# A fused SSM convolution and gated MLP on one core: two spectrum spills moved from the first down phase into the next gate stage, and two chunks of the third gate stage left without convolution steps

## The chip, the core and the metric

The kernel runs on one core of a Trainium2 chip. The metric is the time of one execution on the device in microseconds (us), as a median of several runs. The profile is that of one such execution, taken by the hardware profiler, and it has its own time.

The engines are named as the profile names them: PE is the matrix engine (PEld its weight loads), DVE the vector engine, ACT the scalar engine, POOL the general engine, SP the engine whose instruction queue issues nearly all DMA transfers (SPq in the profile). Each runs its own instructions in order, and they wait for each other through semaphores.

## What is computed

Sequence length 2048, width 576, MLP width 4608, bfloat16 data. Two residual blocks follow one another, both with a layer norm whose scale and shift come from a conditioning vector:

```python
h = layernorm(x) * (1 + ca) + sa
# A: k is shifted and mixed over 4 taps, kv = k_shift * v, then a long causal convolution
y = irfft(rfft(pad(kv)) * rfft(pad(ssm_k)))[:S] + kv * ssm_D
x = x + ga * (h * y)
h = layernorm(x) * (1 + cb) + sb
# B: a gated MLP
x = x + gb * ((silu(h @ w1) * (h @ w3)) @ w2)
```

The convolution is done in blocks of 256 rows, eight of them: block s of the output is a sum over i of (spectrum X of kv block i) times (spectrum V of filter block s - i). The MLP works on four row blocks of 512 rows, each of two convolution blocks.

## The kernel before

**The stages.** `row_blocks` goes over the row blocks r = 0 to 3. For each it runs a gate stage (`stream`; for the last row block `stream_halves`) and then a down phase (`down`). The gate stage computes h @ w1 and h @ w3 for 36 chunks of 128 hidden columns (L1018 and L1029 on PE), puts silu and the copy of the other half on ACT (L1036, L1040) and multiplies them on DVE (L1043). The result lies in `h3`. The down phase multiplies `h3` with w2 (L1139) in two halves of 288 output columns, nine blocks of four hidden chunks in each half, and DVE scales and adds the result to the rows (L1164, L1165).

**The convolution beside it.** While row block r goes through its MLP, the convolution of row block r + 1 is worked off as a list of small steps (the generator `conv`). After each gate chunk, `hide` calls `advance` with a cost, and after each w2 block `down` does so too; `advance` takes as many steps off the list as the sum of the costs allows. In the second half of the down phase (`TURN`), `end` takes all that is left, and the normed rows `h2row` are then transposed by two DMA transposes (L823) into `h2T`, scaled (L838, or L836 on DVE), and are what the next gate stage multiplies with. A layer of the compiler orders the instructions of all engines by their place in the program, so that a step taken later stands later in each engine's queue.

**Spectra.** X (three buffers) and V (four buffers) of the old blocks stay in on-chip memory as long as there are buffers, and are spilled to DRAM for later row blocks: `keep_x(i)` (L446) and `keep_v(i)` (L450) write 864 KB each, `get` (L463) reads one back into the next free buffer. A buffer that is to be used again waits for its last reader and for its spill. In the first down phase of before, four spills are issued, one behind every fourth w2 block: V3, V2, X2, X3. X1, V0 and V1 follow in the gate stage of r = 1, each with the weight load of a group of four chunks (the dictionary `spills`, its keys are those groups).

**Queues.** The w1 and w3 weights (`load_w13`, L969 and L970, 512 KB and 64 KB), the w2 blocks (L1128, 288 KB), spills, reloads, rows and transposes all go through SP's queue. A w2 block goes into one of four places, so its issue waits until PE has done with the block four before it. Each DMA uses one of eight semaphores in turn, so that its issue also waits for the landing of the DMA that used the same one before. Below, w2 blocks of a down phase are counted 0 to 17 over both halves; T1 and T2 are the two transposes of its second half.

PSUM has four accumulators of two banks (`ps`). A gate chunk takes one until ACT has read it, a down half takes two, a spectrum step (L348, copied out by L350) takes one for a moment.

Of the kernel before, what the change touches and what calls it, by code (L numbers as in the profile page):

```python
# [27 lines left out]
W2C = 4  # L28
# [6 lines left out]
HEAD = 8  # L35
HEAD_PACE = 1.4
# [13 lines left out]
class _Kernel:  # L50
# [932 lines left out]
    def stream(self, r, jobs, rate, size, finish=False):  # L983

        nc = self.nc
        hT = self.h2T[r % 2]  # L990
        items = []
        for job in jobs:
            m = RB // (job[2] - job[1])
            items += [(job, fi, m) for fi in range(0, FC, m)]
        gus, ws = {}, {}

        def load(job):
            fc, _, _, buf, also = job
            if fc not in self.w13 and buf is not None:
                if r == 0:  # L1000
                    with self.behind(nc.sync):
                        self.load_w13(fc, buf)
                else:
                    self.load_w13(fc, buf)
            w = self.kept[fc] = self.w13.pop(fc) if buf is not None else self.kept[fc]
            ws[job[0:3]] = w
            if also is not None:
                with self.behind(nc.sync):
                    also()


        def full(k, first):
            (fc, t0, t1, _, _), fi, m = items[k]
            w, n = ws[fc, t0, t1], t1 - t0
            for a in range(m):
                for i in range(2):
                    for ct in range(4):
                        nc.tensor.matmul(gus[k][:, i, a * n:(a + 1) * n],  # L1018
                                         w[:, 5 * i + ct, (fi + a) * P:(fi + a + 1) * P], hT[:, ct, t0:t1],
                                         start=(first and ct == 0 and a == 0),  # L1020
                                         stop=(not first and ct == 3 and a == m - 1))

        def rest(k, first):
            (fc, t0, t1, _, _), fi, m = items[k]
            w, n = ws[fc, t0, t1], t1 - t0
            for a in range(m):
                for i in range(2):
                    rows = slice(64 * i, 64 * i + 64)
                    nc.tensor.matmul(gus[k][:, i, a * n:(a + 1) * n],  # L1029
                                     w[rows, 4, (fi + a) * P:(fi + a + 1) * P], hT[rows, 4, t0:t1],  # L1030
                                     start=(first and a == 0), stop=(not first and a == m - 1))

        def hide(k):
            (fc, t0, t1, _, _), fi, m = items[k]
            f = fc * FC + fi
            nc.scalar.activation(self.h3[:, f:f + m, t0:t1], gus[k][:, 0, :].rearrange("p (a t) -> p a t", a=m),  # L1036
                                 ACT.Silu)
            if k % 2 == 0:
                self.u = self.hp.tile([P, 2, RB], BF16, name="u", tag="u")
            nc.scalar.copy(self.u[:, k % 2, :], gus[k][:, 1, :])  # L1040
            if k % 2 == 1:
                h3 = self.h3[:, f - m:f + m, t0:t1]
                nc.vector.tensor_mul(h3, h3, self.u[:].rearrange("p b (a t) -> p (b a) t", a=m))  # L1043
            del gus[k]
            self.advance(rate * 2.05 * (HEAD_PACE if r == 1 and k < HEAD else 1.0))

        def begin(k):
            if items[k][1] == 0:
                load(items[k][0])
            gus[k] = self.ps()  # L1050
        for k in range(0, len(items), size):
            early, late = range(k, k + size // 2), range(k + size // 2, k + size)
            for m in early:
                begin(m)
                full(m, True)
            for m in early:
                rest(m, False)
            for m in late:
                begin(m)
                rest(m, True)  # L1060
            for m in early:
                hide(m)
            if finish and late.stop == len(items):
                self.end()
            for m in late:
                full(m, False)
                hide(m)
# [50 lines left out]
    def down(self, r, rate):  # L1118
        nc = self.nc
        for h in range(2):  # L1120

            tail = r == NRB - 1 and h == 1
            accs = [self.ps() for _ in range(4 if tail else 2)]
            acc = [accs[t][:, 0, 0:H] if tail else accs[t // 2][:, t % 2, 0:H] for t in range(4)]
            for n, fc in enumerate(FIRST if r == 0 else range(NF // W2C)):
                f0 = n * W2C
                w = _ap(self.w2m, (h * NF + f0) // W2C % NW2 * W2C * H, [[H, W2C], [1, H]])
                nc.sync.dma_start(w, self.w2[fc * W2C * P:(fc + 1) * W2C * P, h * H:(h + 1) * H]  # L1128
                                  .rearrange("(a p) d -> p a d", p=P))
                last = f0 + W2C == NF  # L1130
                if h == 0 and last:
                    self.last_w2 = self.newest()
                order = [(f, t) for f in range(W2C) for t in range(4)]
                if f0 == 0:
                    order = [(f, t) for t0 in (0, 2) for f in range(W2C) for t in (t0, t0 + 1)]
                if last:
                    order = [(f, t) for t in range(4) for f in range(W2C)]
                for f, t in order:
                    nc.tensor.matmul(acc[t],  # L1139
                                     self.h3[:, fc * W2C + f, t * P:(t + 1) * P], w[:, f, :],  # L1140
                                     start=(f0 + f == 0), stop=(f0 + f == NF - 1))
                if h == 1 and f0 // W2C == TURN and r + 1 < NRB:

                    self.end()
                    self.turn_all(2 * r + 3)
                    if 2 * r + 5 < NBLK:
                        self.pair_taps(2 * r + 5)
                    self.modulate(2 * r + 3, r > 0)
                if (f0 // W2C) % 4 == 3:

                    leave = ((self.keep_v, 3), (self.keep_v, 2), (self.keep_x, 2), (self.keep_x, 3)) if r == 0 else ()
                    for keep, i in leave[2 * h + f0 // (4 * W2C):][0:1]:
                        keep(i)
                self.advance(rate * W2C * 4 * 0.126)
            cols = slice(h * H, (h + 1) * H)
            for a in range(2):
                s = 2 * r + a
                x1 = self.xo[s]
                rows = self.out[B * s:B * (s + 1), :].rearrange("(p c) d -> p c d", c=2)
                g = self.lnp.tile([P, 2, H], BF16, name="og", tag="og")  # L1160
                for cc in ((slice(0, 1), slice(1, 2)) if tail else (slice(0, 2),)):
                    n = cc.stop - cc.start
                    ps = acc[2 * a + cc.start].unsqueeze(1) if tail else accs[a][:, :, 0:H]
                    nc.vector.tensor_mul(g[:, cc, :], ps, _ap(self.gbrow, h * H, [[0, n], [1, H]]))  # L1164
                    nc.vector.tensor_add(x1[:, cc, cols], x1[:, cc, cols], g[:, cc, :])  # L1165
                    if r == NRB - 1:
                        nc.sync.dma_start(rows[:, cc, cols], x1[:, cc, cols])
                    elif h == 1:
                        nc.sync.dma_start(rows, x1[:])
# [29 lines left out]
    def row_blocks(self, n1):  # L1199
        for r in range(NRB):  # L1200
            cost = 0
            if r + 1 < NRB:
# [3 lines left out]
                cost = CONV_US[r]  # L1206
            time = 110.0 * 0.85 - (N1 * 1.03 if r == 0 else 0)
            rate = cost / time
            if r == 0:

                jobs = [(fc, 256, 512, None, None) for fc in (n1 - 2, n1 - 1)]

                new = [(n1 + i, 0, RB, b, None) for i, b in enumerate((2, 1, 2))]
                again = [(fc, 256, 512, b, None) for fc, b in enumerate((0, 0, 1, 0))]
                while new or again:
                    jobs += new[0:1] + again[0:1]
                    new, again = new[1:], again[1:]
            else:
                spills = {1: (self.keep_x, 1), 2: (self.keep_v, 0), 4: (self.keep_v, 1)} if r == 1 else {}
                bufs = [b if b == 2 else (r + b) % 2 for b in (0, 1, 2, 0, 1, 2, 0, 1, 0)]  # L1220
                jobs = [(fc, 0, RB, bufs[fc], (lambda f, i: lambda: f(i))(*spills[fc]) if fc in spills else None)
                        for fc in range(NF // FC)]
# [59 lines left out]
```

## Time and profile before

| | |
|---|---|
| median of 5 runs | 509.38 us (508.33 to 510.9) |
| profiled execution | 508.74 us, of which the span from the first to the last instruction is 506.7 us |
| busy in the span | PE 486.8 us (96%), DVE 339.5, ACT 282.3, POOL 22.3 |
| mean granted PE clock | 0.998 |
| DMA | 107.97 MB, mean 213 GB/s |

The stages as the profile shows them, in us from the start of the span: first block and set-up to 90, gate stage of r = 0 to 122.2, its down phase to 164.2, gate stage r = 1 to 241.9, its down phase to 287.6, gate stage r = 2 to 358.4, its down phase to 396.2, then the last gate stage and down phase to the end.

How to read it: a row of the timeline is a run of equal instructions of one engine, with its start, its duration and, in brackets, the idle time before it and what ended that. A PE that is busy is not yet one at its peak, because the ends of matmuls are modelled; but in its gate stages the starts of the matmuls follow each other at a fixed step, and idle time is told in the brackets.

### The profile page before, as it was taken

What the parts mean: (1) busy time and instruction counts of PE and PEld (TensorE: products, weight loads), DVE (VectorE), ACT (ScalarE), POOL (GpSimd) and SP (SyncE); (2) the same over time, 40 slices, a digit from 0 to 9 for tenths busy, and PEclk for the clock granted to TensorE, in tenths of its full rate; (3) what the DMA queues carried; (4) which work ended last, traced back from release to release, by engine and by line L of the source; (5) the groups of instructions that cost most, each with busy time, mean ns of one, the idle gap of its engine ahead of it and who ended that gap; (6) DMA issues with size and microseconds to landing.
All of it is one profiled execution on the core that took longest, in us unless ns stands there. A gap on an engine that the chain in (4) does not pass through costs nothing.

```text
span 506.7 us, 8848 instructions
## 1 busy us (share of the span) xinstructions
PE 486.8 (96%) x3508; PEld 286.2 (56%) x3528; DVE 339.5 (67%) x448; ACT 282.3 (56%) x561; POOL 22.3 (4%) x41
## 2 busy tenths in 40 slices
PE   6999999999998999999999999999999999999996
PEld 3667775547776444343777443434677544444774
DVE  8989898897997576997067999799762321112012
ACT  5658679659243588579450455976824355555000
POOL 4200000000001000000000000000000000000000
PEclk9999999999999999999999999999999999999999
DMA  8988986849999995358799997644575554460562
GB/s 272 337 199 231 320 254 200 246 148 305 266 365 300 296 305 172 105 148 250 202 300 323 313 300 227 209 117 164 152 178 123 172 177 135 148 187 0 141 168 66
DMA packets 115036, 107.97 MB, mean 213 GB/s; under 512 B 20339, under 2 KB 107572, under 8 KB 114996
## 3 DMA queue, kind: packets, MB, share of 16 engines
q1 hardware_dynamic: 114974, 107.41, 71.7%
q8 instruction: 27, 0.44, 0.3%
q14 instruction: 13, 0.11, 0.1%
q10 hardware_dynamic: 22, 0.01, 0.0%
HBM read 92.46 MB, written 9.44 MB: 201 GB/s over the span
## 4 chain that ended last, share of the span: by engine, by line
PE 63%; DVE 17%; DMA 9%; ACT 6%; issue 3%; SPq 1%; POOL 1%; POOLq 0%; DVEq 0%; ACTq 0%
PE ps L1018 27%; PE ps L1139 14%; PE ps L1082 14%; PE ps L1029 4%; DMA wst<-in_B_w_dram 4%; DMA V<-Vd 2%; DVE p L439 2%; DMA kh<-in_A_k_dram 2%; DVE z L441 2%; ACT junk L470 2%; DVE z L434 2%; DVE og L1164 1%; PE ps L348 1%; PE ps L573 1%; DVE h L1043 1%
## 5 line engine op out<-in xcount | busy, mean ns | idle before, releaser
L1018 PE MATMUL ps<-h2T,wst 128*128 128x512 bf16 (+1 forms) x1037 | 198.8, 340 | 1.8 <-issue 0.3
L1139 PE MATMUL ps<-wst,h 128*128 128x288 bf16 x1152 | 145.4, 286 | 5.5 <-DMA wst<-in_B_w_dram 5.1
L1018 PEld LDWEIGHTS <-wst 128*128 128x128 bf16 x1056 | 100.1, 98 | 86.3 <-issue 14.5
L1139 PEld LDWEIGHTS <-h 128*128 128x128 bf16 x1152 | 112.5, 98 | 37.0 <-issue 8.5
L1036 ACT ACTIVATE h<-ps 128x512 bf16<-128x512 f32 x108 | 64.8, 600 | 78.9 <-PE ps L1029 50.8
L1082 PE MATMUL ps<-h2T,wst 64*128 64x512 bf16 x648 | 70.3, 376 | 0.0
L1040 ACT CAST u<-ps 128x512 bf16<-128x512 f32 x108 | 63.3, 586 | 0.0
L439 DVE TENSOR_TENSOR p<-X,V 128x3456 bf16<-128x3456 bf16 x28 | 54.8, 1956 | 3.9 <-DMA V<-Vd 3.4
L441 DVE TENSOR_TENSOR z<-z,p 128x3456 bf16<-128x3456 bf16 x28 | 54.7, 1954 | 0.1
L1082 PEld LDWEIGHTS <-wst 64*128 64x128 bf16 x648 | 31.3, 94 | 38.3 <-DVE og L1164 0.2
L1109 DVE TENSOR_TENSOR h<-h,u 128x1024 bf16<-128x1024 bf16 x18 | 12.5, 692 | 58.1 <-ACT u L1106 58.1
L1043 DVE TENSOR_TENSOR h<-h,u 128x1024 bf16<-128x1024 bf16 x54 | 37.0, 687 | 14.1 <-ACT u L1040 14.1
L1103 ACT ACTIVATE h<-ps 128x512 bf16<-128x512 f32 x36 | 21.5, 597 | 39.9 <-PE ps L1082 39.9
L470 ACT ACTIVATE junk<-x 128x576 bf16<-128x576 bf16 x52 | 35.7, 687 | 3.1 <-DVE x L588 2.6
L1164 DVE TENSOR_TENSOR og<-ps,gbrow 128x576 bf16<-128x576 f32 (+1 forms) x18 | 12.3, 688 | 36.9 <-PE ps L1139 36.4
L1029 PE MATMUL ps<-h2T,wst 64*128 64x512 bf16 (+1 forms) x264 | 33.5, 342 | 0.3
L1106 ACT CAST u<-ps 128x512 bf16<-128x512 f32 x36 | 20.9, 579 | 0.0
L838 ACT ACTIVATE h2T<-h2T,sbcol,cbcol 128x256 bf16<-128x256 bf16 x20 | 10.4, 589 | 18.5 <-DMA h2T<-h2row 18.5
L1029 PEld LDWEIGHTS <-wst 64*128 64x128 bf16 x264 | 8.5, 94 | 21.5 <-issue 18.6
L599 ACT ACTIVATE h2row<-x,l2n,l2r 128x576 bf16<-128x576 bf16 (+1 forms) x24 | 13.7, 642 | 10.2 <-DVE l2n L488 10.2
L368 DVE TENSOR_TENSOR kv<-kv,p 128x1152 bf16<-128x1152 bf16 x24 | 18.1, 756 | 0.3
L362 DVE TENSOR_TENSOR p<-kh,shk 128x3456 bf16<-128x3456 bf16 x8 | 15.6, 1954 | 1.2 <-DMA kh<-in_A_k_dram 1.2
(135 smaller groups left out, 361.4 us busy)
## 6 DMA issues: line engine op xcount, KB each, us to landing
wst<-in_B_w_dram SPq DMA_DIRECT2D x80, 512.0 KB, 5.1
wst<-in_B_w_dram SPq DMA_DIRECT2D x72, 288.0 KB, 3.9
wst<-in_B_w_dram SPq DMA_DIRECT2D x80, 64.0 KB, 3.4
kh<-in_A_k_dram SPq DMA_DIRECT2D x7, 720.0 KB, 6.8
X<-Xd SPq DMA_DIRECT2D x5, 864.0 KB, 5.8
V<-Vd SPq DMA_DIRECT2D x5, 864.0 KB, 5.7
Xd<-X SPq DMA_DIRECT2D x4, 864.0 KB, 8.3
Vd<-V SPq DMA_DIRECT2D x4, 864.0 KB, 5.4
```

Of the source, the lines that this page charges most:

```text
L439: nc.vector.tensor_mul(p[:], X[:], V[:])
L441: nc.vector.tensor_add(z[:], z[:], p[:])
L470: self.nc.scalar.activation(junk[:], src[:, i, :], func, scale=scale, accum_out=out[:, col:col + 1])
L1018: nc.tensor.matmul(gus[k][:, i, a * n:(a + 1) * n], w[:, 5 * i + ct, (fi + a) * P:(fi + a + 1) * P], hT[:, ct, t0:t1], start=(first and ct ...
L1029: nc.tensor.matmul(gus[k][:, i, a * n:(a + 1) * n], w[rows, 4, (fi + a) * P:(fi + a + 1) * P], hT[rows, 4, t0:t1], start=(first and a == 0 ...
L1036: nc.scalar.activation(self.h3[:, f:f + m, t0:t1], gus[k][:, 0, :].rearrange("p (a t) -> p a t", a=m), ACT.Silu)
L1040: nc.scalar.copy(self.u[:, k % 2, :], gus[k][:, 1, :])
L1043: nc.vector.tensor_mul(h3, h3, self.u[:].rearrange("p b (a t) -> p (b a) t", a=m))
L1082: nc.tensor.matmul(gus[k][:, i, :], ws[fc][rows, 5 * i + ct if ct < 4 else 4, cols], hT[rows, ct, :], start=swap == 0 and ct == 4, stop=sw ...
L1103: nc.scalar.activation(h3, gus[k][:, 0, :], ACT.Silu)
L1106: nc.scalar.copy(self.u[:, k % 2, :], gus.pop(k)[:, 1, :])
L1139: nc.tensor.matmul(acc[t], self.h3[:, fc * W2C + f, t * P:(t + 1) * P], w[:, f, :], start=(f0 + f == 0), stop=(f0 + f == NF - 1))
```

## The change

Two spills, those of V2 and X3, leave the down phase of r = 0: two of its four entries are now empty. In the gate stage of r = 1 they are issued with the weights of groups 2 and 3; V0 and V1, which were issued there with groups 2 and 4, now go with groups 5 and 6. X1 stays with group 1.

In the gate stage of r = 2, the last two chunks (34 and 35) take no steps of the convolution any more: their cost is added to the account `due`, and the first `advance` of the down phase takes those steps.

```diff
@@ hide, in stream
             del gus[k]
-            self.advance(rate * 2.05 * (HEAD_PACE if r == 1 and k < HEAD else 1.0))
+            cost = rate * 2.05 * (HEAD_PACE if r == 1 and k < HEAD else 1.0)
+            if r in (2,) and k >= len(items) - 2:
+                self.due += cost
+            else:
+                self.advance(cost)
@@ down
-                    leave = ((self.keep_v, 3), (self.keep_v, 2), (self.keep_x, 2), (self.keep_x, 3)) if r == 0 else ()
-                    for keep, i in leave[2 * h + f0 // (4 * W2C):][0:1]:
+                    leave = ((self.keep_v, 3), (), (self.keep_x, 2), (),) if r == 0 else ()
+                    for keep, i in filter(None, leave[2 * h + f0 // (4 * W2C):][0:1]):
                         keep(i)
@@ row_blocks
-                spills = {1: (self.keep_x, 1), 2: (self.keep_v, 0), 4: (self.keep_v, 1)} if r == 1 else {}
+                spills = {1: (self.keep_x, 1), 2: (self.keep_v, 2), 3: (self.keep_x, 3), 5: (self.keep_v, 0), 6: (self.keep_v, 1)} if r == 1 else {}
```

The number of instructions on every engine stays as it was. In the order of the built programs, these things move beside the edited lines:

- SP, down phase r = 0: the loads of group 1's weights begin behind w2 block 7, where they began behind block 9. X1's spill stands between blocks 10 and 11 (it stood between 11 and 12), X2's stays between 12 and 13. The end of the phase stood as block 16, two of the copies of the filter taps (`kT`, L313), X3's spill, T1, T2, block 17, and X0's reload (L463) behind it. Now it is block 15, X0's reload, block 16, T1, block 17, T2. The loads of k and v rows for the next block (L285, L291) and a filter transpose (L304), which stood behind the weights of group 2, now stand among them.
- PE, down phase r = 0: one L1018 matmul of the next gate stage stood ahead of the last 16 matmuls of the down phase; now all 128 matmuls of the last eight blocks come first.
- DVE: the product of X0 and V4 (L439, L441) moves ahead of the two evictions (L1164) that end this down phase.
- End of gate stage r = 2: on PE, the last chunk's eight L1018 and the first 16 L1139 come before two pairs of L348; on ACT, the last chunk's L1036 and L1040 come before two L534, four L470 and one L350; on SP, T1 of this down phase's first half stands behind three w2 blocks, not two.

## The prediction

> **What bounds the kernel now.** I read the page first, then the stages, then the timelines of PE and SP around the two places that the change touches.
>
> ```profile
> PE 486.8 (96%) x3508; PEld 286.2 (56%) x3528; DVE 339.5 (67%) x448; ACT 282.3 (56%) x561; POOL 22.3 (4%) x41
> ...
> L1139 PE MATMUL ps<-wst,h 128*128 128x288 bf16 x1152 | 145.4, 286 | 5.5 <-DMA wst<-in_B_w_dram 5.1
> ```
>
> PE is the bound, and its waits for w2 blocks are 5.1 us in the whole span: no change to transfers can win much more. Then the stages:
>
> ```profile
> 122.40:164.40 42.00, 38.47 (x307) 29.76 (x305) 37.33 (x44) 18.20 (x36) 2.96 (x2) 1.00 1.11 310
> 164.40:241.90 77.50, 76.97 (x385) 31.85 (x392) 60.53 (x74) 57.64 (x116) 2.50 (x3) 1.00 0.69 212
> ...
> 146.00:154.00 8.00, 5.73 (x46) 4.31 (x45) 7.42 (x10) 3.22 (x10) 2.27 (x1) 1.00 1.05 374
> ```
>
> Columns: window, length, busy time of PE, PEld, DVE, ACT and POOL, granted clock, busy share of the DMA engines, GB/s. In the first down phase DMA is full (1.11). In the gate stage behind it PE is busy for 76.97 of 77.5 us with DMA at 0.69: a time won before 164 is kept there, and a spill put there has room. PE in the down phase:
>
> ```profile
> 135.27 2.12 PE L1139 MATMUL ps<-wst,h 128*128 128x288 bf16 x16 [0.98 <-DMA wst<-in_B_w_dram]
> ...
> 149.66 2.12 PE L1139 MATMUL ps<-wst,h 128*128 128x288 bf16 x16 [0.36 <-DMA wst<-in_B_w_dram]
> 153.69 8.00 PE L1139 MATMUL ps<-wst,h 128*128 128x288 bf16 x64 [1.91 <-DMA wst<-in_B_w_dram]
> 161.97 0.38 PE L1018 MATMUL ps<-h2T,wst 128*128 128x512 bf16 x1 [0.28 <-ACT h2T L838]
> 162.24 2.12 PE L1139 MATMUL ps<-wst,h 128*128 128x288 bf16 x16
> ```
>
> Sixteen matmuls are one w2 block, 1.96 us. Counting by 16, PE waits for blocks 6 (0.98), 12 (0.36) and 13 (1.91); one gate matmul then waits 0.28 for `h2T`, and block 17 follows at 162.24. SP's queue:
>
> ```profile
> 133.02 1.55 SPq L450 DMA_DIRECT2D Vd<-V  x1
> ...
> 153.71 0.53 SPq L446 DMA_DIRECT2D Xd<-X  x1
> 155.36 2.58 SPq L823 DMA_TRANSPOSE h2T<-h2row  x2
> 158.03 0.53 SPq L1128 DMA_DIRECT2D wst<-in_B_w_dram  x1
> ```
>
> V2's spill goes out at 133.02, X3's at 153.71 right ahead of T1 and T2, block 17 last. In the same timeline block 6 is issued at 129.84 and block 13 at 145.16, 8.5 us before PE has it; the page's median for such a block is 3.9.
>
> **Part 1: two spills out of the first down phase.** The wait for block 6 stays: its load was issued 3.2 us before V2's spill. V2 takes 884,736 bytes out of the full stretch, 2.4 us at the 374 GB/s of 146 to 154. Blocks 12 and 13 must come 0.36 and 0.36 + 1.91 = 2.27 us earlier for PE not to wait. The Trainium skill (DMA: Bandwidth & Descriptors, Specifications) gives a ceiling of 435 GB/s, by which the spill is worth 2.0 and 0.3 of wait is left; by the row nothing is left. I take the row, the rate of this very stretch. (X1's spill now stands ahead of block 11, but one spill out and one in leaves its bytes as they were.) So block 16 ends at 153.69 + 8.00 - 2.27 = 159.4.
>
> Late next is block 17. It stands behind T1, which waits for the first row of `h2row`: ACT's L599 started at 153.84, at the end of a DVE chain that did not wait for w2, so it does not move. Half of its 2.29 us gives 155.0, T1's issue 1.26 more, and block 17 goes out at 156.3, not 158.03. With the 3.9 of the page it lands at 160.2, with the 5.8 of block 16 (issued 151.81) at 162.1. I take 160.4, so PE waits 1.0 here in place of 2.27 before, and its 16 matmuls end at 162.4. T2, now behind block 17, goes out at 156.9, 0.2 later than before. It took 4.58 us to land, with X3's spill just ahead; its like in the third down phase took 3.70 and 2.63 with no spill ahead. A rule of the skill speaks against a gain here (same page, Queues, rings and completion order: each DMA engine takes the descriptors of an issuing queue in ring order), so what stands ahead counts, and X0's reload, also 864 KB, comes into the place that X3's spill leaves, some 3 us earlier. By the rows without a spill T2 lands at 160.6, by the rule at 161.5. ACT scales the fourth column tile 2.1 us later, 162.7 or 163.6; PE, started at 162.4, wants it at 163.0. I take 0.3 of loss, the middle. The gate matmuls then count from 162.7; before, their second started at 164.20, so they count from 163.98. **1.3 won**; from -0.3 (block 17 and `h2T` late) to 2.2 (nothing comes in the waits' place).
>
> **What it could cost, each taken at nothing, and its cover.**
> - X0's reload waits for X2's spill (issued 143.4; X1's took 7.2 to land) and holds block 16 and T1 behind it: free at about 151, block 16's place at 151.8. Every us past that is one lost.
> - The DVE product of X0 and V4 ahead of the two evictions: 3.9 us into an idle time of 2.14, so the second eviction is 1.5 later; PE wants that accumulator for its fourth chunk, 6 us into the stage.
> - V2's spill (about 165) must land before DVE writes V5, 178.4 before; landing 5.4.
> - X3's spill stands behind the weights of group 3, whose place is free after four chunks, at 172. It goes at 173 and lands by 182 with the page's 8.3 for such a spill; ACT writes its buffer at 186.6.
> - The row loads behind those weights come at 172, not 167; ACT reads at 180.5.
> - V0 and V1 at groups 5 and 6 meet DMA at 0.69, and weights issued some 15 us before their use; nothing reads them before 250.
>
> Without its cover, ACT or DVE would stand in order and PE with it, us for us.
>
> **Part 2: the end of gate stage r = 2.**
>
> ```profile
> 357.08 1.63 ACT L534 ACTIVATE hg<-x,l1n,l1r 128x576 bf16<-128x576 bf16 x2
> ...
> 359.96 12.78 PE L1139 MATMUL ps<-wst,h 128*128 128x288 bf16 x103 [0.26 <-ACT X L350]
> ...
> 365.37 1.24 SPq L823 DMA_TRANSPOSE h2T<-h2row  x1
> ...
> 373.04 3.22 PE L1139 MATMUL ps<-wst,h 128*128 128x288 bf16 x25 [0.30 <-DMA wst<-in_B_w_dram]
> ```
>
> PE waits 0.26 for an accumulator that a spectrum copy (L350) holds behind L534 and L470 on ACT. With the spectrum matmuls behind the first 16 L1139, both accumulators of the down phase are free: 0.26 won, and the last silu, at 360.48, no longer stands behind them. No instruction is added. The same steps run later: L534 1.63, four L470 at 0.86, two L350 at 0.6 and 1.26 over DVE and POOL, from 359.3 on, put L599 at 366.7, 2.5 later than 364.14. T1 of the first half and its block 7 behind it go with that: T1 at 367.9, block 7 at 369.2. Before, block 7 was held to 369.52 by both transposes. So it lands much as before, the 0.30 at 373.04 stays, and of the 0.26 PE keeps what the earlier issue gives, 0.2. DVE's z is done half a us later, 374, for matmuls at 378.9. **0.2 won**, between -0.5 (blocks 7 and 8 both late behind the transposes) and 0.6.
>
> Sum: 508.74 - 1.3 - 0.2 = 507.2 in the profiled execution. The median, 509.38, lies 0.64 above that execution: **507.8 us**.
>
> **The rivals.**
> - *The wait only moves.* Block 17 and `h2T` end the phase however early blocks 12 and 13 are, since the `h2row` chain stands still; with 162.1 for block 17, part 1 gives nothing and the time is 509.2. For: 1.26 us of T1 stand ahead of block 17. Against: it is issued 1.7 us earlier than before.
> - *All of the w2 waits behind V2 go.* Landings of 3.9 and 3.7: 2.2 + 0.6, 506.6.
> - *X3's spill becomes ACT's wait (slower).* At about 186 ACT's copy of spectrum X4 needs X3's buffer, and silus and PSUM copies queue behind it. The spill is behind SP's waits for PE and for V2's landing. It decides from a landing after 186 + 1.5; to be 2 us slower in all (511.4) it must land at 190, 17 us after my issue time. Against: that is twice the page's 8.3.
> - *It changes nothing measurable* because the reload of X0 gives back V2's 2.4 us: 509.
>
> **How the numbers follow.** A measurement of this kernel tells about 0.3% (1.5 us) from no change, so the bounds are 507.85 and 510.9, and my sum lies on the first. Chances: the sum as worked 0.4, all waits gone 0.2, the wait moves or is given back 0.22, X3's spill or another cover that fails 0.18. Half of the first and the whole of the second give faster, 0.40; the last gives slower, 0.18; the same has 0.42. The range goes from 506.0 (the upper ends of both parts, 505.94 + 0.64 = 506.6, and 0.6 of spread, the shown runs lying within 1.5 of their median) to 510.6, which takes in the whole of the moved wait and stops short of the slower case, about 0.15, with 0.05 left out below.
>
> **What would show it.** Right: no wait at blocks 12 and 13, the 0.98 at block 6 unchanged, a wait of about 1 at block 17, the gate stage counted from 162.7, 77.5 us long as before, no wait for L350 at 360. Wrong: waits at 12 or 13 still over 0.5, T1 issued after 155.5, a PE gap between 165 and 200 behind ACT or DVE, or L599 in the third down phase later than 367 with PE waiting over 0.6 at block 7 or 8.

## The result, and the profile after

| | before | after |
|---|---|---|
| median | 508.98 us (506.87 to 511.14, 40 runs) | 505.36 us (504.33 to 508.63, 21 runs) |
| profiled execution, span | 508.74 us, 506.7 us | 505.74 us, 503.9 us |

The ratio is 0.9938, 95% interval 0.9923 to 0.9953: 3.2 us won (2.4 to 3.9). The prediction was 507.8 us with a range from 506.0 to 510.6; the measured median lies 0.6 below that range. Faster was given 0.40, the same 0.42; by the bound of 0.3% that the prediction set for itself, this is faster. The median of before, now over 40 runs, lies 0.4 under the 509.38 that the prediction counted from.

In the costliest groups of the page of after, the lines L1128, L1139 and L1164 of before are L1132, L1143 and L1168:

```profile
PE 486.2 (96%) x3508; PEld 286.0 (57%) x3528; DVE 338.9 (67%) x448; ACT 282.4 (56%) x561; POOL 22.7 (4%) x41
...
L1143 PE MATMUL ps<-wst,h 128*128 128x288 bf16 x1152 | 145.4, 286 | 3.6 <-DMA wst<-in_B_w_dram 3.5
```

PE's busy time is the same to 0.6 us and its waits for w2 blocks fell from 5.1 to 3.5. The windows by stage of after (first down phase, the gate stage behind it, and the same 8 us that the prediction took its rate from; columns as there):

```profile
121.82:160.89 39.07, 37.87 (x306) 29.72 (x304) 36.80 (x42) 17.50 (x36) 2.96 (x2) 1.00 1.12 305
160.89:238.61 77.72, 77.19 (x386) 31.89 (x392) 60.32 (x75) 58.41 (x118) 2.50 (x3) 1.00 0.74 226
146.00:154.00 8.00, 7.47 (x62) 5.83 (x61) 7.42 (x12) 3.25 (x9) 2.27 (x1) 1.00 1.10 337
```

The phase is 39.07 us and not 42.00. DMA is still full in it (1.12), so a transfer that is wanted soon can still be late there. Between 146 and 154, where PE was busy for 5.73 us of 8, it is now busy for 7.47. The gate stage is as long as before, if before is counted from 163.98 as the prediction did: 77.72 there too. PE in the first down phase, by its timeline:

```profile
121.82 11.92 PE L1143 MATMUL ps<-wst,h 128*128 128x288 bf16 x96
134.00 2.12 PE L1143 MATMUL ps<-wst,h 128*128 128x288 bf16 x16 [0.25 <-DMA wst<-in_B_w_dram]
...
143.94 8.00 PE L1143 MATMUL ps<-wst,h 128*128 128x288 bf16 x64
152.48 4.08 PE L1143 MATMUL ps<-wst,h 128*128 128x288 bf16 x32 [0.53 <-DMA wst<-in_B_w_dram]
156.97 4.08 PE L1143 MATMUL ps<-wst,h 128*128 128x288 bf16 x32 [0.42 <-DMA wst<-in_B_w_dram]
160.89 1.89 PE L1018 MATMUL ps<-h2T,wst 128*128 128x512 bf16 x7
```

The 64 matmuls at 143.94 are blocks 10 to 13 without a stop: both waits that the prediction wanted gone are gone. Smaller ones came at blocks 14 and 16. Block 17 and the first gate matmuls wait for nothing. The wait at block 6 is 0.25, not 0.98. SP's queue at the end of the phase:

```profile
149.03 1.38 SPq L463 DMA_DIRECT2D X<-Xd  x1
150.51 0.39 SPq L1132 DMA_DIRECT2D wst<-in_B_w_dram  x1
153.79 1.21 SPq L823 DMA_TRANSPOSE h2T<-h2row  x1
155.10 0.53 SPq L1132 DMA_DIRECT2D wst<-in_B_w_dram  x1
155.72 1.21 SPq L823 DMA_TRANSPOSE h2T<-h2row  x1
...
163.92 0.57 SPq L450 DMA_DIRECT2D Vd<-V  x1
```

X0's reload goes out at 149.03 (before: 160.22), T1 at 153.79 and block 17 at 155.10. The prediction had both 1.2 us later, but PE, too, is 1.27 us earlier in this profile: block 9 starts at 141.74, in before at 143.01. And the end of the third gate stage on PE:

```profile
356.19 2.12 PE L1143 MATMUL ps<-wst,h 128*128 128x288 bf16 x16
358.15 0.65 PE L348 MATMUL ps<-kv,Fb 128*128 128x288 bf16 x4
358.64 17.56 PE L1143 MATMUL ps<-wst,h 128*128 128x288 bf16 x142
```

The spectrum matmuls (L348) stand behind the first block. Neither the wait for L350 nor the one for block 7 is there any more.

**Waits counted by steps.** From here on a wait is the time from one matmul's start to the next one's, less 0.12 us for each matmul, since 16 of them take 1.96 us from start to start. That is more than the idle time in brackets: an x16 row is shown with 2.12 us where the next row can start after 1.96, so each bracket leaves out 0.16 us. The first down phase is cut at the start of block 9, since up to block 7 nothing moves in the order of SP's instructions. Lengths in us from the profiled executions ("gate" is counted 0.22 earlier where one L1018 runs ahead of the last block, as it does in before):

| kernel | start to block 9 | block 9 to gate | gate r = 1 | gate r = 2 with its down phase |
|---|---|---|---|---|
| before | 20.77 | 20.97 | 77.73 | 115.52 |
| before again (e6) | 20.26 | 21.00 | 77.72 | 115.24 |
| steps only (e2) | 20.98 | 22.28 | 77.77 | 114.65 |
| X3 only (e4) | 19.51 | 20.64 | 77.72 | 115.89 |
| V2 only (e3) | 20.17 | 18.87 | 78.61 | 115.14 |
| V2 split (e12) | 20.36 | 18.92 | 78.01 | 115.07 |
| both spills (e1) | 19.72 | 19.00 | 77.72 | 115.67 |
| no spill (e8) | 19.87 | 18.85 | 77.72 | 115.24 |
| after | 19.92 | 19.15 | 77.72 | 114.65 |
| after again (e5) | 20.00 | 18.61 | 77.88 | 114.65 |
| after, X1 too (e7) | 20.74 | 18.61 | 77.94 | 114.70 |
| after, early 17 (e9) | 20.07 | 18.93 | 77.72 | 114.74 |
| X1 too, early 17 (e10) | 19.94 | 18.07 | 77.72 | 114.70 |
| and steps r = 1 (e11) | 19.51 | 17.88 | 77.72 | 114.60 |

The profiled pair differs by 2.8 us in span. By the table: 0.85 before block 9, 1.82 from there to the gate stage, 0.87 in the stretch of part 2. The stages ahead of the change are 0.42 shorter in after, and the second down phase is 1.22 longer (it waits 2.7 us in all for w2 blocks, before 1.5). Sum: 0.85 + 1.82 + 0.87 + 0.42 - 1.22 = 2.74.

### The profile page after: what moved, and what is told of

It reads as the page before. It is cut to its first block, busy times and chain, and to the rows that moved or that the text cites. A ratio compares the mean times of both kernels' runs of the same rounds, so it can differ in the third digit from the quotient of the medians.

```text
span 503.9 us, 8848 instructions
## 1 busy us (share of the span) xinstructions
PE 486.2 (96%) x3508; PEld 286.0 (57%) x3528; DVE 338.9 (67%) x448; ACT 282.4 (56%) x561; POOL 22.7 (4%) x41
## 4 chain that ended last, share of the span: by engine, by line
PE 64%; DVE 17%; DMA 9%; ACT 4%; issue 3%; SPq 1%; POOL 0%; POOLq 0%; DVEq 0%; ACTq 0%
PE ps L1018 27%; PE ps L1143 15%; PE ps L1086 14%; PE ps L1029 4%; DMA wst<-in_B_w_dram 4%; DMA V<-Vd 3%; DVE p L439 2%; DMA kh<-in_A_k_dram 2%; DVE z L441 2%; ACT junk L470 2%; DVE z L434 2%; DVE og L1168 2%; PE ps L348 1%; PE ps L573 1%; DVE h L1043 1%
## 5 line engine op out<-in xcount | busy, mean ns | idle before, releaser
L1018 PE MATMUL ps<-h2T,wst 128*128 128x512 bf16 (+1 forms) x1037 | 198.6, 340 | 1.6 <-issue 0.3
L1018 PEld LDWEIGHTS <-wst 128*128 128x128 bf16 x1056 | 100.1, 98 | 86.8 <-issue 15.0
L1143 PE MATMUL ps<-wst,h 128*128 128x288 bf16 x1152 | 145.4, 286 | 3.6 <-DMA wst<-in_B_w_dram 3.5
L1143 PEld LDWEIGHTS <-h 128*128 128x128 bf16 x1152 | 112.5, 98 | 34.7 <-issue 5.7
L1036 ACT ACTIVATE h<-ps 128x512 bf16<-128x512 f32 x108 | 64.8, 600 | 79.0 <-PE ps L1029 49.8
L1040 ACT CAST u<-ps 128x512 bf16<-128x512 f32 x108 | 63.4, 587 | 0.0
L439 DVE TENSOR_TENSOR p<-X,V 128x3456 bf16<-128x3456 bf16 x28 | 54.7, 1955 | 3.8 <-DMA V<-Vd 3.4
L441 DVE TENSOR_TENSOR z<-z,p 128x3456 bf16<-128x3456 bf16 x28 | 54.7, 1953 | 0.1
L470 ACT ACTIVATE junk<-x 128x576 bf16<-128x576 bf16 x52 | 35.7, 687 | 3.1 <-DVE x L588 2.6
L1168 DVE TENSOR_TENSOR og<-ps,gbrow 128x576 bf16<-128x576 f32 (+1 forms) x18 | 12.3, 688 | 34.1 <-PE ps L1143 33.6
L599 ACT ACTIVATE h2row<-x,l2n,l2r 128x576 bf16<-128x576 bf16 (+1 forms) x24 | 13.8, 654 | 12.5 <-DVE l2n L488 12.5
```

Source lines behind the costliest of these rows:

```text
L439: nc.vector.tensor_mul(p[:], X[:], V[:])
L441: nc.vector.tensor_add(z[:], z[:], p[:])
L470: self.nc.scalar.activation(junk[:], src[:, i, :], func, scale=scale, accum_out=out[:, col:col + 1])
L1018: nc.tensor.matmul(gus[k][:, i, a * n:(a + 1) * n], w[:, 5 * i + ct, (fi + a) * P:(fi + a + 1) * P], hT[:, ct, t0:t1], start=(first and ct ...
L1143: nc.tensor.matmul(acc[t], self.h3[:, fc * W2C + f, t * P:(t + 1) * P], w[:, f, :], start=(f0 + f == 0), stop=(f0 + f == NF - 1))
```

## The experiments

The diffs here are cuts: lines that are as in the change above, and definitions, are left out.

**e1 and e2: each part alone.** Theory: part 1 carries the gain. Rival: part 2 does, or the two only work together. e1 is the changed kernel with the old `advance` in `hide`; e2 is the kernel before with the new one:

```diff
+            if r in (2,) and k >= len(items) - 2:
+                self.due += cost
+            else:
+                self.advance(cost)
```

> The change without its second part: the last two chunks of gate stage r = 2 take their convolution steps as before. Theory A (the first down phase gives nearly all): ratio to before about 0.995 (2.6 us won), the first down phase in its profile about 39.1 us, as in the changed kernel, and PE's wait of 0.26 for L350 at the start of the third down phase back. Theory B (part 1 was sized right at 1.3 us and part 2 gives the rest): ratio about 0.9975, first down phase 40.5 us or more.

> The second part alone: spills as before, the last two chunks of gate stage r = 2 without convolution steps. Theory A: ratio 0.999 (0.5 us won), third down phase 37.2 us, where before has 37.7, nothing else moved. Theory B: ratio 0.996 or lower (2 us won).

Measured: e1 506.42 us, ratio 0.9955 (0.9938 to 0.9973); e2 508.18 us, 0.9995 (0.9974 to 1.0016); before 508.63. Part 1 is most of the gain, 2.3 us. PE of e1 and then of e2, from the timelines:

```profile
152.26 4.08 PE L1139 MATMUL ps<-wst,h 128*128 128x288 bf16 x32 [0.28 <-DMA wst<-in_B_w_dram]
156.83 4.08 PE L1139 MATMUL ps<-wst,h 128*128 128x288 bf16 x32 [0.49 <-DMA wst<-in_B_w_dram]
...
356.26 12.82 PE L1139 MATMUL ps<-wst,h 128*128 128x288 bf16 x103 [0.26 <-ACT X L350]
```

```profile
150.38 2.12 PE L1143 MATMUL ps<-wst,h 128*128 128x288 bf16 x16 [0.41 <-DMA wst<-in_B_w_dram]
154.50 9.67 PE L1143 MATMUL ps<-wst,h 128*128 128x288 bf16 x64 [1.99 <-DMA wst<-in_B_w_dram]
...
361.63 17.92 PE L1143 MATMUL ps<-wst,h 128*128 128x288 bf16 x144
```

e1 has after's waits at blocks 14 and 16 and keeps before's wait for L350; e2 keeps before's waits at 12 and 13 (its x64 at 154.50 takes 9.67 us and not 8.00, a further wait of 1.67 at block 14) and loses the one for L350. The times don't resolve part 2: 0.3 us won by e2, with an interval from 1.3 won to 0.8 lost. The profiles do, in the last column of the table: the seven profiles with part 2 have 114.60 to 114.74, the seven without 115.07 to 115.89. The means are 114.67 and 115.40, so part 2 is worth 0.73 us in its stretch.

**e3 and e4: which spill.** Theory: V2's bytes are what delays blocks 12 and 13, and X3's spill matters little for PE. Rival: X3's, ahead of T1 and T2.

```diff
 e3  leave = ((self.keep_v, 3), (), (self.keep_x, 2), (self.keep_x, 3),) if r == 0 else ()
 e3  spills = {1: (self.keep_x, 1), 2: (self.keep_v, 2), 5: (self.keep_v, 0), 6: (self.keep_v, 1)} if r == 1 else {}
 e4  leave = ((self.keep_v, 3), (self.keep_v, 2), (self.keep_x, 2), (),) if r == 0 else ()
 e4  spills = {1: (self.keep_x, 1), 3: (self.keep_x, 3), 5: (self.keep_v, 0), 6: (self.keep_v, 1)} if r == 1 else {}
```

> V2's spill leaves the first down phase, X3's stays in it (now between blocks 15 and 16); V0 and V1 at groups 5 and 6; no second part. If V2's bytes are what delayed blocks 12 and 13: no wait for them, ratio about 0.997 (1.5 us), with X3's spill in front of T1, T2 and block 17 these late and a wait of about 1 us at the phase's end. If the place of X3 at the end is what counts: ratio 0.999 or more.

> X3's spill leaves the first down phase, V2's stays where it was; V0 and V1 at groups 5 and 6; no second part. If V2's bytes delay blocks 12 and 13: both waits stay (0.36 and 1.91), ratio 0.998 to 1.0, only T2 and block 17 land sooner (T2 in 3.4 to 3.7 us, not 4.58), which PE cannot use. If the end of the phase was the bound: ratio 0.996.

Measured: e3 506.56 us, 0.9959 (0.9943 to 0.9974); e4 508.05 us, 0.9993 (0.9974 to 1.0012). The gain of part 1 comes with V2's spill. PE of e3, then of e4:

```profile
153.24 8.20 PE L1139 MATMUL ps<-wst,h 128*128 128x288 bf16 x64 [0.63 <-DMA wst<-in_B_w_dram]
...
168.63 0.41 PE L348 MATMUL ps<-kT,Fk 128*128 128x288 bf16 x2 [0.67 <-DVE og L1164]
```

```profile
148.23 2.12 PE L1139 MATMUL ps<-wst,h 128*128 128x288 bf16 x16 [0.30 <-DMA wst<-in_B_w_dram]
152.49 9.96 PE L1139 MATMUL ps<-wst,h 128*128 128x288 bf16 x80 [2.14 <-DMA wst<-in_B_w_dram]
```

With V2 in place the waits at 12 and 13 stay (e4); with V2 gone they go (e3). That it is V2's own bytes is not shown by this, because the queue changes behind the spill. SP's queue in before and then in after:

```profile
141.61 0.58 SPq L446 DMA_DIRECT2D Xd<-X  x1
142.96 0.37 SPq L1128 DMA_DIRECT2D wst<-in_B_w_dram  x1
143.37 0.57 SPq L446 DMA_DIRECT2D Xd<-X  x1
```

```profile
137.82 0.58 SPq L446 DMA_DIRECT2D Xd<-X  x1
...
142.11 0.50 SPq L446 DMA_DIRECT2D Xd<-X  x1
```

V2's spill goes out at 133.02 in before, ten us ahead of block 12; by the page's median of 5.4 us for such a spill, or the 7.2 of X1's, it had landed 4.5 or 2.7 us before block 12 went out (an estimate). What stands right ahead of blocks 12 and 13 are the spills of X1 and X2, 1.6 to 1.8 us apart in all four profiles with V2 in place. In the seven that have X1's spill in this phase, but not V2's or only an eighth of it, they are 4.1 to 4.3 us apart, with two blocks between them. So V2's spill may delay these blocks by its bytes or by pushing X1's up against X2's; no run has one without the other.

The wait of about 1 us that was expected of e3 at the end of the phase did not come: by the step it waits 0.79 at block 14 and 0.20 at block 16, and nothing at 17. e3 also shows what X3's move is good for. Its line at 168.63 is a wait of PE in the gate stage that neither before nor after has. DVE of e3 and then of after, around the two evictions:

```profile
162.86 1.96 DVE L439 TENSOR_TENSOR p<-X,V 128x3456 bf16<-128x3456 bf16 x1 [2.19 <-DMA X<-Xd]
...
167.82 0.76 DVE L1164 TENSOR_TENSOR og<-ps,gbrow 128x576 bf16<-128x576 f32 x1
```

```profile
159.92 1.95 DVE L439 TENSOR_TENSOR p<-X,V 128x3456 bf16<-128x3456 bf16 x1
...
164.88 0.76 DVE L1168 TENSOR_TENSOR og<-ps,gbrow 128x576 bf16<-128x576 f32 x1
```

In e3 X3's spill still stands in the queue, so X0's reload is issued at 157.67 and DVE stands 2.19 us in order for it. The second eviction comes at 167.82, and PE wants its accumulator earlier: 0.67 us idle, and with it the gate stage takes 78.61 us in the table where after has 77.72. (e12, where X3's spill stays as well, has 78.01.) With X3 gone the reload goes out at 149.03 and the eviction is done at 165.64, before PE's L348 at 167.35. The times of e1 and e3 do not differ, so this is a reading of the profiles.

**e5 and e6: both kernels again, unchanged.** How much of the pair's difference is chance?

> The changed kernel once more, for a second profile and for comparison on the same chip. Theory A (gain in the first down phase by V2 alone): ratio 0.993 to 0.996, no wait at blocks 12 and 13, waits of together about 1.3 us at blocks 14 and 16 as in its first profile. If the wait of block 6 differs from one execution to the next and is no matter of the change, it lies anywhere from 0 to 1.2 us here (0.25 in the first profile).

> The kernel before once more, for a second profile. If block 6's wait of 0.98 us belongs to the kernel, it is 0.9 to 1.1 again; if it is chance of the execution, anything from 0 to 1.2. The waits at blocks 12 and 13 (0.36 and 1.91) are there again in both cases, and the chain from the inverse transform's matmuls (L573) to L599 takes 14.4 us again, whatever block 6 did.

Measured: e5 504.55 us, 0.9928 (0.9901 to 0.9955); e6 508.17 us in its one run. PE of e6, the kernel before:

```profile
135.39 2.12 PE L1139 MATMUL ps<-wst,h 128*128 128x288 bf16 x16 [0.21 <-DMA wst<-in_B_w_dram]
149.82 2.12 PE L1139 MATMUL ps<-wst,h 128*128 128x288 bf16 x16 [0.40 <-DMA wst<-in_B_w_dram]
154.23 8.00 PE L1139 MATMUL ps<-wst,h 128*128 128x288 bf16 x64 [2.29 <-DMA wst<-in_B_w_dram]
```

The wait at block 6 was 0.98 in one execution of the same program and is 0.21 here; e4, with the same order up to there, has none. Those at 12 and 13 come again. So the 0.85 us before block 9 in the pair are largely scatter: profiles with V2 in place have 19.51 to 20.98 there (mean 20.4), those without 19.51 to 20.74 (mean 20.0). Whether 0.4 of it belongs to the change stays open. The column behind it is steady: 20.64 to 22.28 with V2 in place, 17.88 to 19.15 without.

**e7, e9, e10, e11: the waits that came in the place.** What holds blocks 14 and 16 in after? Theory: X1's spill, which now stands ahead of block 11 in the same full stretch. Rival: block 17 behind T1 is the next bound anyway. e7 moves X1's spill to group 4. e9 issues block 17 ahead of T1 and T2 (`block` holds the issue of a w2 block, taken out of the loop). e10 does both. e11 does both and takes part 2's edit for r = 1 as well.

```diff
 e7   spills = {2: (self.keep_v, 2), 3: (self.keep_x, 3), 4: (self.keep_x, 1), 5: (self.keep_v, 0), 6: (self.keep_v, 1)} if r == 1 else {}
 e9   if h == 1 and f0 // W2C == TURN and r + 1 < NRB:
+         early = block(n + 1)
          self.end()
 e11  if r in (1, 2) and k >= len(items) - 2:
```

> The changed kernel with X1's spill, too, out of the first down phase: it goes with group 4 in the gate stage. If the waits left at blocks 14 and 16 are bytes in front of them, X1's 864 KB gone 10 us earlier win up to 1.0 us: ratio 0.991 to 0.993. If X2's spill and X0's reload alone make them, the same as the changed kernel, 0.994.

> The changed kernel, with w2 block 17 issued ahead of T1 and T2 (before the turn) in the down phases of r = 0 to 2. If what is left at the end of these phases is block 17 behind T1: no wait for block 17 in any of them, some 0.4 us won in each of the last two (0.39 at the end of the third in the profile of the changed kernel) and up to 0.5 in the first; ratio 0.990 to 0.992. If blocks 14 and 16 and the scaled h2T are what ends the phase: as the changed kernel, 0.993 to 0.994.

> The same, and X1's spill out of the first down phase, as in the run that moved X1 alone. Moving X1 took the waits at blocks 14 and 16 away and put 0.7 us at block 17 in their place; with block 17 ahead of T1 both are gone: first down phase 38.0 us, ratio 0.989 to 0.990. If h2T, which hangs on the chain from L573, is late next, PE waits for L838 instead and the ratio stays at 0.992 or above.

> The same, and the last two chunks of gate stage r = 1 take no convolution steps either. If the switch at the end of a gate stage is worth 0.2 to 0.4 us wherever it is: another 0.05% off the run before. If the steps of r = 1 are on the path of the second down phase, which waits for reloaded V and X: 0.5 to 1 us slower than that run, with longer waits on DVE there.

Measured: e7 505.07 us, 0.9941 (0.9924 to 0.9958); e9 504.48 us, 0.9926 (0.99 to 0.9951); e10 504.61 us, 0.994 (0.9914 to 0.9967); e11 503.93 us, 0.9921 (0.9895 to 0.9948). PE of e7, of e9 and of e10:

```profile
144.73 13.88 PE L1143 MATMUL ps<-wst,h 128*128 128x288 bf16 x112
159.17 2.12 PE L1143 MATMUL ps<-wst,h 128*128 128x288 bf16 x16 [0.56 <-DMA wst<-in_B_w_dram]
```

```profile
151.97 4.08 PE L1149 MATMUL ps<-wst,h 128*128 128x288 bf16 x32 [0.31 <-DMA wst<-in_B_w_dram]
156.45 4.08 PE L1149 MATMUL ps<-wst,h 128*128 128x288 bf16 x32 [0.40 <-DMA wst<-in_B_w_dram]
```

```profile
144.63 16.03 PE L1149 MATMUL ps<-wst,h 128*128 128x288 bf16 x128
```

In e7 blocks 10 to 16 run through and block 17 waits 0.56 (0.73 by the step): X1's spill was the cause at 14 and 16 (SP's queue in this phase has otherwise the same order in e7 and after), and behind it stands the bound that the prediction named. So e7 gives at block 17 what it wins before: its stretch of 18.61 us is that of e5, and the ratio of 0.991 to 0.993 that was expected did not come. e9 alone changes nothing there, since in after block 17 is not the late one. Nor does it help the third down phase, where 0.4 us was expected: there the last block still goes out behind T1 and T2 (at 385.68, T2 at 384.31), and waits 0.48 by the step, in after 0.39. With both, e10 runs blocks 10 to 17 in one row, and the stretch takes 18.07 us, or 17.88 in e11 where nothing waits. The times cannot tell this gain, 1.1 us against after and 0.5 against e5: all four intervals overlap with that of after. e11's own question, whether the last two chunks of r = 1 are worth something too, stays open: its second down phase takes 38.87 us, e10's 38.28, and over all profiles this phase scatters by 2 us.

**e8: are the moved spills free where they are now?** As e1, with the two spills left out in the gate stage, so that V3 and X2 are read back in their place.

```diff
+        i = {("V", 2): 3, ("X", 3): 2}.get((which, i), i)
-  spills = {1: (self.keep_x, 1), 2: (self.keep_v, 2), 3: (self.keep_x, 3), 5: (self.keep_v, 0), 6: (self.keep_v, 1)} if r == 1 else {}
+  spills = {1: (self.keep_x, 1), 5: (self.keep_v, 0), 6: (self.keep_v, 1)} if r == 1 else {}
```

> The spills of V2 and X3 are left out altogether, and where V2 and X3 are read back, V3's and X2's are read instead; no second part. It tells what the two spills cost in the gate stage. If nothing (all covers hold): ratio as with the two spills moved and no second part, 0.9955, gate stage r = 1 at 77.7 us as there. If they cost there: ratio 0.993 or lower and a shorter gate stage.

Measured: 505.58 us, 0.9952 (0.9932 to 0.9971), where e1 had 0.9955. The gate stage's window of e1 and then of e8:

```profile
160.75:238.47 77.72, 77.72 (x395) 31.88 (x393) 60.46 (x75) 58.53 (x118) 2.51 (x3) 1.00 0.74 227
```

```profile
160.76:238.49 77.73, 77.73 (x395) 31.85 (x393) 60.50 (x75) 58.60 (x119) 2.50 (x3) 1.00 0.67 204
```

DMA moves 227 or 204 GB/s, and PE has no gap either way: in this stage the two spills cost nothing.

**e12: an eighth of V2 left where it was.** As e3, with 432 of V2's 3456 columns written at the old place (`part_v` writes the columns given to it), to see whether the cost goes with the bytes or with the issue.

```diff
-  leave = ((self.keep_v, 3), (), (self.keep_x, 2), (self.keep_x, 3),) if r == 0 else ()
+  leave = ((self.keep_v, 3), (lambda i: self.part_v(i, 0, 432), 2), (self.keep_x, 2), (self.keep_x, 3),) if r == 0 else ()
-  spills = {1: (self.keep_x, 1), 2: (self.keep_v, 2), 5: (self.keep_v, 0), 6: (self.keep_v, 1)} if r == 1 else {}
+  spills = {1: (self.keep_x, 1), 2: (lambda i: self.part_v(i, 432, 3456), 2), 5: (self.keep_v, 0), 6: (self.keep_v, 1)} if r == 1 else {}
```

> As with V2's spill alone moved, but an eighth of V2 (108 KB) is still written at the old place, the rest at group 2. If the bytes delay blocks 12 and 13: an eighth of them is 0.3 us, so the ratio of the run without it, 0.996, or 0.0005 above, and waits of at most 0.5 at blocks 12 and 13. If it is that a transfer stands there at all (its issue, its semaphore): 0.999 and the waits of before.

Measured: 506.62 us, 0.9963 (0.9945 to 0.9982), e3 had 0.9959. Block 9 to the gate stage takes 18.92 us, e3 18.87. So an eighth of the bytes, with one more DMA in the queue, costs nothing that can be seen: it is not the issue that delayed blocks 12 and 13. But the queue behind it has the order of e3, with the spills of X1 and X2 4.1 us apart, so bytes and order are not separated here either. How the wait grows between an eighth and all of V2 was not tried.

## Why the prediction was too small

The places were right: the gain comes where the two parts act. Two terms of the sum were too small, the waits at blocks 12 and 13 (2.27, measured 2.59) and part 2 (0.2, measured 0.73 to 0.87), and the 3.2 us by the times (2.4 to 3.9) are twice the 1.5 of the sum.

- **"Blocks 12 and 13 must come 0.36 and 0.36 + 1.91 = 2.27 us earlier": 0.3 too small.** The waits went when V2 went (e3, not e4), as predicted; that V2's bytes did it, at the rate of the stretch, is not shown. But 0.36 + 1.91 are brackets; by the steps they cost 0.52 + 2.07 = 2.59. That is more than the 2.4 at which the prediction priced V2's bytes, and yet nothing was left of it.
- **What comes in their place: size right, place wrong.** The prediction lost 1.3 at the end of the phase in place of 0.33 before, a wait of 1.0 at block 17 and 0.3 for `h2T`. The run lost 0.69 at block 14 and 0.58 at block 16, 1.27 in sum, and nothing at 17 or `h2T`. That the sums agree is luck; in e5 the same stretch loses 0.73. Before had 0.49 at that end by the step. So block 9 to the gate stage won 2.59 + 0.49 - 1.27 = 1.81, where the prediction had 2.27 + 0.33 - 1.3 = 1.3. The table has 1.82 for this pair, and 2.39 for e5 against e6.
- **"X1's spill now stands ahead of block 11, but one spill out and one in leaves its bytes as they were": did not look far enough.** Block 11 does not wait, but by e7 that spill is what made blocks 14 and 16 wait.
- **"At the end of a DVE chain that did not wait for w2, so it does not move" (L599): it moved, but not against PE.** The chain starts from PE. Before and then after, from the timelines:

```profile
139.43 1.14 PE L573 MATMUL ps<-z,Fb 128*128 128x288 bf16 x8
...
153.84 2.29 ACT L599 ACTIVATE h2row<-x,l2n,l2r 128x576 bf16<-128x576 bf16 x4 [4.68 <-DVE l2n L488]
```

```profile
138.16 1.14 PE L573 MATMUL ps<-z,Fb 128*128 128x288 bf16 x8
...
152.57 2.29 ACT L599 ACTIVATE h2row<-x,l2n,l2r 128x576 bf16<-128x576 bf16 x4 [4.68 <-DVE l2n L488]
```

  From L573 to L599 it is 14.40 to 14.41 us in all fourteen profiles, and L573 stands behind block 7 on PE. A chain that waits for w2 nowhere along its own way still moves with the blocks ahead of its first link. Here that is the 1.27 us by which all of PE up to block 9 was earlier, which is mostly scatter (see e5 and e6). Counted from block 9, block 17 went out at 13.36 us, and the prediction had it at 13.3. It did not wait, because blocks 14 and 16 had held PE back by 1.27: by the 3.6 us that the page of after has for such a block, 17 landed at 158.7 (an estimate), and PE wanted it at 158.93. Where those two waits are gone (e7), block 17 waits 0.73. So this bound was real; the prediction had the landing 0.7 us too late (17.39 us after block 9, by e7 16.65).
- **T2 and the rule of ring order.** The prediction set the rows without a spill ahead (T2 lands at 160.6, 3.7 us after its issue) against what it drew from the ring order that the Trainium skill states (DMA: Bandwidth & Descriptors, Queues, rings and completion order): 161.5, 4.6 us after. It took the middle. T2 was issued at 155.72 and landed 3.35 us later: the row was right. The run does not speak against the rule: X0's reload, issued at 149.03, took 7.0 us, so it had landed 0.3 us after T2's issue and was hardly ahead of it. Where 864 KB ahead did count is at blocks 14 and 16, and these were X1's (e7).
- **"The wait for block 6 stays": failed as a number.** It was 0.98 in one execution and 0.21 in the next of the same kernel (e6). The pair's 0.85 us before block 9 is mostly this.
- **Part 2, 0.2: failed in size; 0.87 in the pair, 0.73 as a mean of seven profiles each.** The wait for L350 is worth 0.43 by the step, not 0.26. And the 0.30 at block 7, which "stays", is gone, 0.46 by the step. Of the seven profiles without part 2, before, e1 and e4 wait 0.46 to 0.61 there and e8 0.21; of the seven with it only e2 has a wait there, 0.12. What runs later was placed right: L599 starts 8.33 us behind the start of this down phase, before 5.71, so 2.6 later where 2.5 was said. Block 7 goes out at 10.87 us, 10.8 by the prediction. Only the landing was put too late; what brings it earlier was not found.
- **The covers held.** X0's reload went out at 149.03 and held up nothing. No wait of PE is seen between 161 and 200: X3's spill goes out at 173.48, and ACT writes its buffer at 183.52. The slower rival found nothing to stand on. The one cover with little to spare is the second eviction: e3, where the reload is late, pays 0.9 us there.
- **"All of the w2 waits behind V2 go", 506.6 and 0.2 of the chance,** is nearest to what was measured, by luck: the waits at 14 and 16 are still there, and what was missing from the brackets and at block 7 made up for them.
- **The range** took its lower end from upper ends worked out with the same brackets. With the median of before at 508.98 and the sum of the two steady columns, 20.98 - 18.88 (means of two profiles each) + 0.73 = 2.8, the time would be 506.2. The other 0.8 us to 505.36 is not accounted for; it is within the interval of the ratio, whose upper end, 0.9953, gives 506.6.

## What to carry to other kernels

Take the cost of a wait from the start of one instruction to the start of the next, not from the idle time in brackets, and read a wait in two executions before a sum leans on it. When a transfer is moved out of a full stretch, ask of each chain that is said to stand still which instruction starts it, and count its times from there. Look, too, at what the transfer pushed back while it was in the queue, and at the next bulk transfer ahead of the loads that are wanted soon: here X1's spill followed V2's. A spill that delays PE by 2 us in a phase with full DMA costs nothing in a stage with DMA at 0.74 and a deep lead of weights.

## What the runs showed of the hardware

- The same program waits differently at the same place from one execution to the next while DMA is full: 0.98 and 0.21 us at block 6, and 38.07 to 40.15 us for the second down phase over all profiles, with no relation to the change that can be seen.
- An x16 row of matmuls is shown as 2.12 us, but the next row follows after 1.96 where nothing waits: each bracket of idle time before a matmul leaves out 0.16 us.
- The full stretch from 146 to 154 moved 374 GB/s before and 337 after, with DMA at 1.05 and 1.10: the rate that a spill's bytes were priced at is not a constant of the stretch.
- In the gate stage of r = 1 two spills of 864 KB more or less (227 and 204 GB/s, DMA at 0.74 and 0.67) leave PE's time the same: 77.72 us in e1 and e8.
